# One partial sum of exponentials per half and head in place of two, in a bucketed-attention and rational-FFN kernel

## The chip, the cores and the metric

The kernel runs on one core of a Trainium2 chip. The metric is the device time of one execution in microseconds (us), as the median of several runs. Engines are called as the profile calls them: PE (TensorE), DVE (VectorE), ACT (ScalarE), POOL (GpSimd) and SP (SyncE, which issues DMAs).

## What is computed

Attention in which a query sees only the keys of its own hash bucket, and then a feed-forward layer whose nonlinearity is a quotient of polynomials. There are 4 batches, 8 heads, 768 positions and head size 64, so 3072 tokens of 512 features; the hidden layer has 2048.

```python
mask = q_bucket[:, :, :, None] == k_bucket[:, :, None, :]     # 6 sign bits of q @ proj, k @ proj
scores = scale * np.matmul(q, k.transpose(0, 1, 3, 2))
scores = np.where(mask, scores, -1000000000.0)
scores = scores - np.max(scores, axis=-1, keepdims=True)
attn = np.exp(scores)
attn = attn / (np.sum(attn, axis=-1, keepdims=True) + 1e-09)
x = np.matmul(attn, v)                                        # then heads side by side
...
h = x @ w_in
P = a[0] + a[1] * h + a[2] * h2 + a[3] * h3
Q = 1.0 + np.abs(b[0]) * np.abs(h) + np.abs(b[1]) * h2
out = (P / (Q + 1e-6)) @ w_out
```

The change concerns `np.sum(attn, axis=-1)`, the sum of the exponentials over the keys.

## The kernel before

Two heads make a pair; 16 pairs go through attention one after the other, with the work of neighbouring pairs interleaved. A pair has 12 steps: two halves of 384 queries, and in each half six key tiles of 128 keys. Keys lie on the partitions and queries along the free axis.

- `scores(p, s)` does one step. For each head PE makes two products into a PSUM tile (`pss`), ACT takes the exponential into a tile E (seven such tiles, used in turn, each for both heads), and POOL adds the tile to a running sum `acc`.
- `values(p, s)` multiplies a step's E with V into `psv`. In most pairs the six steps of a half go in one group behind its last scores.
- `maxstep(p, j)` makes maxima of the scores for a pair two places ahead: two products on PE (`psm`), one TENSOR_REDUCE on DVE (`m`). Its PSUM tiles come from the pool `ps_a`, which has two buffers; the bucket bits (`psb` on PE, compared on DVE into `mb`, for two pairs at a time) use the same two.
- `sums(p)` multiplies the running sums with a matrix of ones (`psu`), so that the sum over 128 partitions comes out on PE; a column group of 32 columns takes one head and half. ACT copies the result to `sr`.
- `low` (tiles `lo`) splits q and k into two parts for exact products, `weights(i)` prepares the FFN's weights a tile at a time (`wr`, `ws`, `wi_hi`, `wi_lo`, two tiles a pair); most of their arithmetic is on DVE.
- Behind attention comes the FFN (`psh`, `pso` on PE, `gl` on POOL); from there on POOL has no adds of exponentials.

The order on every engine is the program's own. It is written by a table: `at(p, s, f, ...)` puts a piece of work at a place counted in steps of pair p, and all pieces are issued sorted by place. The sums of a pair stand at 14.65 (pair 14: 14.69, pair 15: 16.96), that is 2.65 steps into the next pair, behind the `psm` of that step.

`PARTS` says into how many partial sums the six key tiles of a half go, `ACCS` how many buffers `acc` has. With PARTS = 2 the tiles 0 to 2 go into one sum and 3 to 5 into another. The lines that use them:

```python
        n = NT // PARTS                                        # NT = 6 key tiles
        if kt % n == 1 and heads[0] == 0:
            ACC[p, hf, kt // n] = sm.tile([P, 2, HQ], F32, tag="acc", ..., bufs=ACCS)
        if kt % n > 0:
            acc = ACC[p, hf, kt // n]
            x = EXP[p, s - 1] if kt % n == 1 else acc
            for h in heads:
                engine = nc.vector if h and late >= LAST["share"] else nc.gpsimd
                engine.tensor_tensor(out=acc[:, h, :], in0=x[:, h, 0:HQ], in1=e[:, h, 0:HQ], op=ALU.add)
...
        for k in range(PARTS):                                 # in sums(p)
            for hf in range(2):
                ...
                    nc.tensor.matmul(ps[o : o + 32, 0:HQ], ones, acc[:, h, :], start=(k == 0), stop=(k == PARTS - 1))
```

From the last step of pair 14 on (`late >= LAST["share"]`), DVE adds head 1 and POOL only head 0.

Of the kernel before, what the change touches and what calls it, by code (L numbers as in the profile page):

```python
# [34 lines left out]
BIG = 2.0 ** 60  # L35
CLAMP = 2.0 ** 40
PINNED = ("tensor", "vector", "scalar", "gpsimd", "sync")
PARTS = 2
ACCS = 5

MID = dict(
    group=6, values=[0.66, 0.05], values_out=[0.69, 0.06],
# [132 lines left out]
def attention(ctx, tc, nc, raw, ps_b, tail, tokens, early, operands_to_terms, ffn, load, QF, KF, v, w_in, w_out, wo_d, ident, cst, ones, prj,  # L175
# [180 lines left out]
    def scores(p, s, heads=(0, 1)):  # L356
# [13 lines left out]
        if both is not None:  # L370
            for h in heads:
                nc.scalar.activation(e[:, h, 0:HQ], both[:, h, 0:HQ], AF.Exp, scale=1.0 / 8.0)
        n = NT // PARTS
        if kt % n == 1 and heads[0] == 0:
            ACC[p, hf, kt // n] = sm.tile([P, 2, HQ], F32, tag="acc", name=f"acc{p}_{hf}_{kt // n}", bufs=ACCS)
        if kt % n > 0:
# [25 lines left out]
    def sums(p):  # L402
        ps = ps_b.tile([P, 512], F32, tag="s", bufs=3, name=f"psu{p}")
        for k in range(PARTS):
            for hf in range(2):
                acc = ACC.pop((p, hf, k))
                for h in range(2):
                    o = 64 * h + 32 * hf
                    nc.tensor.matmul(ps[o : o + 32, 0:HQ], ones, acc[:, h, :], start=(k == 0), stop=(k == PARTS - 1))
        ACC[p] = tail.tile([P, DM], F32, tag="sr", name=f"sr{p}")[:, 0:HQ]  # L410
# [437 lines left out]
```

## Time and profile before

| | |
|---|---|
| time of the runs | 924.08 us median of 3 (923.99 to 924.12) |
| span of the profiled execution, first to last instruction | 921.5 us |
| time around the span, median less span | 2.6 us |
| PE busy | 915.5 us, 99% |
| DVE busy | 841.5 us, 91% |
| ACT busy | 653.8 us, 71% |
| POOL busy | 426.3 us, 46% |

The profiled execution's own device time isn't listed apart from the runs, so its span stands for it. A row of the timeline gives start, length, engine, line, operation, what is written and what is read, how many instructions are merged, and in brackets the idle time of the engine before it with what ended it. Instructions are all recorded at line 95, a helper, so rows are told apart by their tiles (buffer numbers left out). A matmul in full fp32 precision appears as two records, and the ends of matmuls are modelled, so PE rows are read by their starts.

### The profile page before, as it was taken

The page shows a single profiled execution, that of the slowest core. Times are in us where ns is not written, and L with a number is a line of the kernel's source. Part 1 is how long each engine was busy: PE and PEld are TensorE (multiplying, and loading weights), DVE is VectorE, ACT ScalarE, POOL GpSimd, SP SyncE. Part 2 cuts the span into 40 slices and gives each one's busy share as a digit, 9 for nine tenths or more (in the row PEclk, how much of TensorE's full clock was granted, in tenths as well). Part 3 has the DMA queues.
Part 4 walks back from the last instruction along what each step waited for, and adds up shares of the span by engine and source line. Part 5 has one row for each costly group of instructions (what it writes and reads, how often), then busy time and mean ns, then how long its engine had stood idle before and what let it go on. Part 6 is the DMA issues. An engine that isn't in the chain of part 4 may idle for free.

```text
span 921.5 us, 13665 instructions
## 1 busy us (share of the span) xinstructions
PE 915.5 (99%) x4671; PEld 699.2 (76%) x4671; DVE 841.5 (91%) x1022; ACT 653.8 (71%) x1227; POOL 426.3 (46%) x363
## 2 busy tenths in 40 slices
PE   9999999999999999999999999999999999999998
PEld 5567767676767676678888888888888888888886
DVE  6799989999899899788998999999999989998997
ACT  7467777777777776976767677767676777667664
POOL 7577777677777777712222222222222222322221
PEclk9999999999999999999999999999999999999999
DMA  7877878787878778555403000400040013001001
GB/s 205 210 214 224 234 205 240 219 236 214 240 209 235 199 213 242 158 191 163 138 1 108 31 1 1 137 1 0 1 137 1 1 43 95 1 1 46 1 0 47
DMA packets 51242, 111.57 MB, mean 121 GB/s; under 512 B 9346, under 2 KB 20214, under 8 KB 51172
## 3 DMA queue, kind: packets, MB, share of 16 engines
q1 hardware_dynamic: 50740, 110.47, 40.7%
q8 instruction: 37, 0.61, 0.3%
q14 instruction: 33, 0.27, 0.1%
q10 hardware_dynamic: 432, 0.23, 0.1%
HBM read 56.82 MB, written 21.17 MB: 85 GB/s over the span
## 4 chain that ended last, share of the span: by engine, by line
PE 99%; DVE 1%; issue 0%; ACT 0%; DVEq 0%
PE psh L95 28%; PE pso L95 28%; PE pss L95 15%; PE psv L95 14%; PE psm L95 8%; PE psu L95 2%; PE psb L95 1%; PE psw L95 1%; PE pst L95 0%; PE pst_None L95 0%; PE psb_first L95 0%; DVE m L95 0%; DVE ws L95 0%; DVE k L95 0%; DVE mb L95 0%
## 5 line engine op out<-in xcount | busy, mean ns | idle before, releaser
L95 POOL TENSOR_TENSOR gl<-c,gh 128x512 fp32r<-128x512 f32 x95 | 135.8, 1429 | 384.9 <-ACT gh L95 374.8
L95 PE MATMUL pso<-wo,gh 128*128 128x512 f32 x768 | 235.9, 389 | 0.0
L95 DVE TENSOR_REDUCE m<-psm 128x1 f32<-128x768 f32 x192 | 181.3, 953 | 28.7 <-PE psm L95 20.1
L95 ACT ACTIVATE E<-pss 128x384 f32<-128x384 f32 x384 | 167.1, 492 | 41.5 <-PE pss L95 33.5
L95 POOL TENSOR_TENSOR acc<-E,E 128x384 f32<-128x384 f32 x124 | 147.2, 1206 | 92.1 <-ACT E L95 92.1
L95 PE MATMUL pss<-q,k 128*128 128x384 f32 (+2 forms) x768 | 171.0, 346 | 0.2
L95 PEld LDWEIGHTS pso<-wo,gh 128*128 128x128 f32 x768 | 144.1, 188 | 29.9
L95 ACT ACTIVATE h<-psh 128x512 f32<-128x512 f32 x96 | 57.4, 598 | 133.1 <-PE psh L95 133.0
L95 PEld LDWEIGHTS pss<-q,k 128*128 128x128 f32 (+2 forms) x768 | 134.5, 190 | 21.3 <-issue 8.0
L95 PE MATMUL psh<-xh,wi_hi 128*128 128x512 f32 x384 | 149.6, 390 | 0.0
L95 PE MATMUL psh<-xl,wi_hi 128*128 128x512 f32 x384 | 149.4, 389 | 0.0
L95 PE MATMUL psh<-xh,wi_lo 128*128 128x512 f32 x384 | 149.4, 389 | 0.0
L95 PE MATMUL pso<-wo,gl 128*128 128x512 f32 x384 | 148.9, 389 | 0.0
L95 DVE SCALAR_TENSOR_TENSOR c<-c,ab,r 128x512 f32<-128x512 f32 x96 | 138.7, 1444 | 0.0
L95 POOL TENSOR_TENSOR acc<-acc,E 128x384 f32<-128x384 f32 x123 | 132.0, 1093 | 3.8 <-ACT E L95 3.4
L95 PE MATMUL psv<-E,v 128*64 128x385 f32 x768 | 131.9, 492 | 0.0
L95 PE MATMUL psm<-k,q 76*128 76x384 f32 (+1 forms) x384 | 101.0, 345 | 0.5 <-ACT q L95 0.2
L95 PEld LDWEIGHTS psv<-E,v 128*64 128x64 f32 x768 | 52.0, 137 | 65.1 <-issue 62.4
L95 DVE SCALAR_TENSOR_TENSOR w<-h,absb,w 128x512 f32<-128x512 f32 x96 | 72.8, 758 | 15.5 <-ACT w L95 15.2
L95 PEld LDWEIGHTS psh<-xh,wi_hi 128*128 128x128 f32 x384 | 72.0, 188 | 16.1 <-issue 1.2
L95 PEld LDWEIGHTS psh<-xl,wi_hi 128*128 128x128 f32 x384 | 72.1, 188 | 15.0
L95 PEld LDWEIGHTS pso<-wo,gl 128*128 128x128 f32 x384 | 72.1, 188 | 15.0
(77 smaller groups left out, 1212.9 us busy)
## 6 DMA issues: line engine op xcount, KB each, us to landing
q<-q SPq DMA_DIRECT2D x45, 192.0 KB
k<-k SPq DMA_DIRECT2D x45, 192.0 KB
wr<-w_in SPq DMA_DIRECT2D x16, 512.0 KB
wr<-w_out SPq DMA_DIRECT2D x16, 512.0 KB
wo_d<-wr SPq DMA_DIRECT2D x16, 512.0 KB
wo<-wo_d SPq DMA_DIRECT2D x16, 512.0 KB
qkf<-qT SPq DMA_DIRECT2D x16, 384.0 KB
qkf<-kT SPq DMA_DIRECT2D x16, 384.0 KB
```

What stands on the lines that cost most here:

```text
L95: return self.tc.keep_in_program_order(issue(*args, **kwargs))
```

## The change

`PARTS` becomes 1 and `ACCS` 3. All six key tiles of a half go into one sum, by five adds for each half and head in place of four, and `sums` makes one product for each half and head in place of two.

```diff
-PARTS = 2
-ACCS = 5
+PARTS = 1
+ACCS = 3
```

On PE, this is the order at the sums of pair 6 before. In `acc6_1_0` the numbers are pair, half and partial sum, and "x2" stands for both heads; `psm8` are maxima for pair 8 and `pss7` scores of pair 7.

```order
L95 MATMUL psm8_8_2343<-k1_8_2045,q1_8_1990 128x384 x2
L95 MATMUL psu6_2348<-acc6_0_0_2036,ones_80 32x384 x2
L95 MATMUL psu6_2348<-acc6_1_0_2195,ones_80 32x384 x2
L95 MATMUL psu6_2348<-acc6_0_1_2116,ones_80 32x384 x2
L95 MATMUL psu6_2348<-acc6_1_1_2248,ones_80 32x384 x2
L95 MATMUL pss7_3_0_2364<-q1_7_1717,k1_7_1771 128x384
```

And this is the same place of the changed kernel:

```order
L95 MATMUL psm8_8_2333<-k1_8_2037,q1_8_1982 128x384 x2
L95 MATMUL psu6_2338<-acc6_0_0_2028,ones_80 32x384 x2
L95 MATMUL psu6_2338<-acc6_1_0_2184,ones_80 32x384 x2
L95 MATMUL pss7_3_0_2350<-q1_7_1711,k1_7_1765 128x384
L95 MATMUL pss7_3_0_2350<-q2_7_1941,k2_7_1942 128x384
```

Nothing moved on PE: the four products of the second partial sums are gone, and the neighbours are as they were.

On POOL, these are the adds of pair 6 before, E0 to E6 being the seven tiles of exponentials:

```order
L95 TENSOR_TENSOR acc6_0_0_2036<-E2_149,E3_150 128x384 x2
L95 TENSOR_TENSOR acc6_0_0_2036<-acc6_0_0_2036,E4_151 128x384 x2
L95 TENSOR_TENSOR acc6_0_1_2116<-E5_152,E6_153 128x384 x2
L95 TENSOR_TENSOR acc6_0_1_2116<-acc6_0_1_2116,E0_147 128x384 x2
L95 TENSOR_TENSOR acc6_1_0_2195<-E1_148,E2_149 128x384 x2
L95 TENSOR_TENSOR acc6_1_0_2195<-acc6_1_0_2195,E3_150 128x384 x2
L95 TENSOR_TENSOR acc6_1_1_2248<-E4_151,E5_152 128x384 x2
L95 TENSOR_TENSOR acc6_1_1_2248<-acc6_1_1_2248,E6_153 128x384 x2
```

And these are the adds of pair 6 in the changed kernel:

```order
L95 TENSOR_TENSOR acc6_0_0_2028<-E2_149,E3_150 128x384 x2
L95 TENSOR_TENSOR acc6_0_0_2028<-acc6_0_0_2028,E4_151 128x384 x2
L95 TENSOR_TENSOR acc6_0_0_2028<-acc6_0_0_2028,E5_152 128x384 x2
L95 TENSOR_TENSOR acc6_0_0_2028<-acc6_0_0_2028,E6_153 128x384 x2
L95 TENSOR_TENSOR acc6_0_0_2028<-acc6_0_0_2028,E0_147 128x384 x2
L95 TENSOR_TENSOR acc6_1_0_2184<-E1_148,E2_149 128x384 x2
L95 TENSOR_TENSOR acc6_1_0_2184<-acc6_1_0_2184,E3_150 128x384 x2
L95 TENSOR_TENSOR acc6_1_0_2184<-acc6_1_0_2184,E4_151 128x384 x2
L95 TENSOR_TENSOR acc6_1_0_2184<-acc6_1_0_2184,E5_152 128x384 x2
L95 TENSOR_TENSOR acc6_1_0_2184<-acc6_1_0_2184,E6_153 128x384 x2
```

The fourth tile of a half (E5, then E4) was not added by itself before, but together with the fifth; now every tile after the first has an add of its own, at the place of its step.

## The prediction

> **What bounds the kernel now.** I read the page first (busy shares and the chain), then one window over twelve pairs, then the PE timeline around one sum of exponentials.
>
> ```profile
> PE 915.5 (99%) x4671; PEld 699.2 (76%) x4671; DVE 841.5 (91%) x1022; ACT 653.8 (71%) x1227; POOL 426.3 (46%) x363
> PEclk9999999999999999999999999999999999999999
> PE 99%; DVE 1%; issue 0%; ACT 0%; DVEq 0%
> ```
>
> PE is busy all the time, at a full granted clock, and the chain that ended last is 99% PE. The 46% of POOL (GpSimd) is an average over two stages. The stage that matters is attention; this window runs from the sums of pair 1 to those of pair 13.
>
> ```profile
> 75.58:357.24 281.66, 281.66 (x1741) 198.32 (x1740) 253.82 (x292) 206.52 (x451) 213.47 (x193) 1.00 0.79 223
> ```
>
> Columns: window, then busy time of PE, PEld, DVE, ACT, POOL. By twelfths a pair takes 23.47 us. PE fills it, DVE works 21.15 of it (2.32 idle) and GpSimd 17.79 (5.68 idle). So time taken from PE is worth its full length until DVE or GpSimd has no idle time left, and both are nearer to that here than the page's shares say.
>
> **What is removed.** The PE timeline at the sums of pair 4 (the third row is from a narrower window, the last from the groups):
>
> ```profile
> 146.60 1.50 PE L95 MATMUL psu<-acc,ones 128*32 128x384 f32 x16
> 148.03 0.80 PE L95 MATMUL pss<-q,k 77*128 77x384 f32 x3
> 147.59 0.51 PE L95 MATMUL psu<-acc,ones 128*32 128x384 f32 x4
> L95 PE MATMUL psu<-acc,ones 128*32 128x384 f32 x256 | 24.0, 492 | 0.1
> ```
>
> Sixteen matmul records (eight products of two records) run in four rounds of four, one in each 32-column group. The rounds start from 146.60 to 147.59, so 0.33 apart; the next scores begin at 148.03. The change keeps two rounds: 2 x 0.33 = 0.66 less a pair, say 0.65. Half of the whole group (24.0 / 2 = 12.0 us over 16 pairs) is the other bound, 0.75 a pair, but entering and leaving the group isn't halved. I take 16 x 0.65 = **10.4 us**, with 12.0 as the ceiling. Weight loads for the removed products lie beside the matmuls.
>
> **What is added: GpSimd.** A half and head has five adds instead of four, so a pair has 20 instead of 16: four of its eight `E+E` become `acc+E`, and four `acc+E` come new. The groups give the mean prices:
>
> ```profile
> L95 POOL TENSOR_TENSOR acc<-E,E 128x384 f32<-128x384 f32 x124 | 147.2, 1206 | 92.1 <-ACT E L95 92.1
> L95 POOL TENSOR_TENSOR acc<-acc,E 128x384 f32<-128x384 f32 x123 | 132.0, 1093 | 3.8 <-ACT E L95 3.4
> ```
>
> Four more adds at the mean of both, 1.15, make 17.79 + 4.6 = 22.4 us of GpSimd in a pair that PE would do in 23.47 - 0.65 = 22.82. It fits, with 0.4 to spare; the break-even price of an added add is (22.82 - 17.79) / 4 = **1.26 us**. Where the adds go is seen in GpSimd's timeline over two halves, with the PE row of pair 6's sums:
>
> ```profile
> 181.96 1.97 POOL L95 TENSOR_TENSOR acc<-E,E 128x384 f32<-128x384 f32 x2 [3.47 <-ACT E L95]
> 187.62 2.46 POOL L95 TENSOR_TENSOR acc<-acc,E 128x384 f32<-128x384 f32 x2
> 192.58 3.17 POOL L95 TENSOR_TENSOR acc<-E,E 128x384 f32<-128x384 f32 x2 [2.51 <-ACT E L95]
> 200.16 2.46 POOL L95 TENSOR_TENSOR acc<-acc,E 128x384 f32<-128x384 f32 x2
> 204.85 2.01 POOL L95 TENSOR_TENSOR acc<-E,E 128x384 f32<-128x384 f32 x2 [2.23 <-ACT E L95]
> 193.63 1.50 PE L95 MATMUL psu<-acc,ones 128*32 128x384 f32 x16
> ```
>
> The idle time stands between the halves: 3.47, 2.51, 2.23. The second half of pair 6 ends at 190.08, and its sums start on PE at 193.63: 3.55 of slack. With two adds more (1.97 without interference, 3.17 at the dearest) it ends at 192.05 to 193.25, still ahead of its sums, and ahead of the next half's first E at 192.58 in the likely case. The first half of pair 7 ends at 202.62 and then at about 204.7, against 204.85. So no queue builds up from pair to pair, and PE doesn't wait at the sums: cost nothing, covered by the 3.55. An E buffer is written again seven steps later, more than a half's six, so ScalarE isn't held. Three ACC buffers serve two live sums and one being made; the one used again was read by the sums half a pair earlier. The smaller pool moves later tiles in SBUF; its cost I put at nothing, since the first w_out tile is wanted only four FFN steps on.
>
> **What is slowed: DVE.** In GpSimd's idle time VectorE prepares weights. Here is one such step without GpSimd, the same under it, and the spread of these operations (lowest, median, highest in ns):
>
> ```profile
> 178.97 0.68 DVE L95 SCALAR_TENSOR_TENSOR ws<-ws,wr 128x512 int32<-128x512 int32 x1
> 201.82 1.35 DVE L95 SCALAR_TENSOR_TENSOR ws<-ws,wr 128x512 int32<-128x512 int32 x1
> L95 DVE SCALAR_TENSOR_TENSOR ws<-ws,wr x32: 676/1232/1469, 44.8 to 393.8; 128x512 int32<-128x512 int32 x32
> L95 DVE CUSTOM_DVE_ANT_0 ws<-wr,ws x32: 668/681/1296, 48.3 to 394.6; 128x1024 uint16<-128x1024 uint16 x32
> L95 DVE TENSOR_SCALAR wr<-wr x32: 414/469/1099, 32.1 to 393.3; 128x512 int32<-128x512 int32 x32
> L95 DVE TENSOR_TENSOR wr<-ws,wr x16: 680/1414/1498, 55.2 to 396.0; 128x512 fp32r<-128x512 f32 x16
> ```
>
> The two engines hold each other up. Two of each of the first three run in a pair. Bounds of what DVE gains in work: nothing, if they all still find gaps; and 2 x (1.469 - 0.676 + 1.296 - 0.668 + 1.099 - 0.414) = 4.2 us, if each goes from its lowest to its highest. Some are under GpSimd already, and four of 5.68 idle us go away; I take a fifth of that, 0.8 a pair: 21.15 + 0.8 = 22.0 of 22.82. DVE still fits on average. It doesn't at one place, the sums that are followed by the bucket bits `psb` (pair 5; DVE rows, then PE):
>
> ```profile
> 166.22 0.69 DVE L95 SCALAR_TENSOR_TENSOR ws<-ws,wr 128x512 int32<-128x512 int32 x1
> 167.44 0.96 DVE L95 TENSOR_REDUCE m<-psm 128x1 f32<-128x768 f32 x1 [0.54 <-PE psm L95]
> 171.52 0.95 DVE L95 TENSOR_TENSOR lo<-qkf,k 128x768 fp32r<-128x768 f32 x1
> 172.38 1.01 DVE L95 TENSOR_SCALAR mb<-psb,cst 128x768 fp32r<-128x768 f32 x1
> 173.55 3.09 DVE L95 TENSOR_REDUCE m<-psm 128x1 f32<-128x768 f32 x3 [0.16 <-PE psm L95]
> 170.78 1.47 PE L95 MATMUL psb<-qkf,prj 128*32 128x384 f32 x16
> 174.07 0.52 PE L95 MATMUL psm<-k,q 76*128 76x384 f32 x2
> ```
>
> From 167.44 to 173.39 DVE has no idle time. The maxima `psm` at 174.07 take the PSUM buffer that `mb` leaves at 173.39: 0.68 of slack, which PE's 0.65 uses up. Whatever makes DVE late here is then lost on PE. The `ws` at 166.22 ran alone and is covered now: about 0.67 later (1.35 - 0.68), its neighbours some tenths, less 0.54 of idle time ahead of 167.44: 0.4 late. Six sums (odd pairs 1 to 11) have `psb` behind them: 6 x 0.4 = **2.4 us** lost, between 0 and 6 x 0.65 = 3.9.
>
> **Pair 14.** Here DVE takes the last add of head 1, and the sums come close behind:
>
> ```profile
> 375.13 1.00 POOL L95 TENSOR_TENSOR acc<-acc,E 128x384 f32<-128x384 f32 x1
> 375.20 1.35 DVE L95 TENSOR_TENSOR acc<-acc,E 128x384 f32<-128x384 f32 x1 [1.87 <-POOL acc L95]
> 377.36 1.50 PE L95 MATMUL psu<-acc,ones 128*32 128x384 f32 x16
> ```
>
> Two GpSimd adds more stand ahead of that DVE add, which begins near 377.2 and ends near 378.5; PE would want it at 377.4 or so. PE waits about a microsecond, the saving there is gone: **1.0 us** lost (0.3 to 2). Queued behind it on DVE is weight work, which nothing on PE wants soon. Pair 15 has two more DVE adds, at most 1.35 each, well ahead of its sums in the FFN.
>
> **The sum.** 10.4 - 2.4 - 1.0, and 13 x 0.15 = 2.0 for places where two queues at 96 to 98% of their pair catch on each other (0 to 0.4 each; a guess between these): 5.0 us. The profiled span is 921.5; 916.5 after. The median of the runs, 924.08, lies 2.6 above the span, work outside the first and last instruction that the change leaves: **919.1 us**. A measurement here tells 0.2%, 1.9 us, from no change.
>
> **Rivals.** *Full gain:* DVE's slowing is absorbed and only pair 14 loses: about 9 to 10 us, 914.5. For it: DVE's 2.3 idle us a pair; against: the 0.68 at `mb`. *No change:* DVE is a microsecond late at the odd sums and several tenths at the others, and the 10.4 is eaten: 922.5 to 925.5.
>
> *Slower, GpSimd becomes the bound.* Past 1.26 us for an added add, GpSimd's lateness grows from pair to pair until PE waits at every sums for the last add. The dearest adds of the rows cost 3.17 / 2 = 1.59: 17.79 + 4 x 1.59 = 24.15 a pair, 0.68 over 23.47, over 13 pairs 9 us: 933. For it: 0.4 us of margin only; against: the added adds mostly fall where the old ones cost 0.97.
>
> *Slower, DVE is shut out.* This row shows an operation held through three adds:
>
> ```profile
> 210.05 2.88 DVE L95 TENSOR_TENSOR wi_lo<-ws,wi_hi 128x512 fp32r<-128x512 f32 x1
> ...
> L95 DVE TENSOR_TENSOR wi_lo<-ws,wi_hi x16: 677/1053/2885, 70.4 to 392.7; 128x512 fp32r<-128x512 f32 x16
> ```
>
> The median of this operation is 1.05 (below). If GpSimd's longer unbroken runs did this once a pair, DVE would have 21.15 + 0.8 + 1.8 = 23.75 us to do: 0.28 over, 13 x 0.28 = 4 us slower, 928. It happened once in the whole trace.
>
> *Slower, full exclusion.* If GpSimd's adds (0.98 each, from 1.97 for two) and VectorE's operations on SBUF (lowest prices 0.68, 0.67, 0.41, 0.68 and 0.95 for `lo`, two of each a pair: 6.8) could not overlap at all, a pair would take 20 x 0.98 + 6.8 = 26.4 us, 2.9 more than now, 38 us over 13 pairs: 962. Against it stands what VectorE did under the eight adds from 192.58 to 202.62:
>
> ```profile
> 192.48 0.68 DVE L95 CUSTOM_DVE_ANT_0 ws<-wr,ws 128x1024 uint16<-128x1024 uint16 x1
> 193.94 0.94 DVE L95 TENSOR_TENSOR lo<-qkf,q 128x768 fp32r<-128x768 f32 x1
> 197.29 1.08 DVE L95 TENSOR_TENSOR lo<-qkf,k 128x768 fp32r<-128x768 f32 x1
> 200.02 0.47 DVE L95 TENSOR_SCALAR wr<-wr 128x512 int32<-128x512 int32 x1
> 200.41 1.48 DVE L95 TENSOR_TENSOR wr<-ws,wr 128x512 fp32r<-128x512 f32 x1
> ```
>
> At lowest prices these are 3.7 us. The adds took 10.04, 2.2 more than 8 x 0.98: six tenths of it was paid, and in the gaps between halves nothing is. The Trainium skill, "SBUF — State Buffer", section "Who interferes with whom", has the rule: a VectorE instruction with two SBUF inputs and a GpSimd instruction that reads SBUF block each other, the later for the whole of the earlier. By that rule the sum is this rival's; the trace agrees in kind (0.68 against 1.35 for `ws`), and not in full size.
>
> **Chances.** Forecast (gain 3 to 8) 0.52; full gain 0.13; no change 0.17; GpSimd bound 0.09; DVE shut out 0.06; full exclusion 0.03. Faster by over 0.2%: the first two and a little of the third's edge, 0.67; within: 0.15; slower: 0.18. The forecast's own range is 916 to 921.5. For eight in ten the range goes from the full gain, 914.3, into the milder slower cases, 927.
>
> **What would show it.** `psu` at 128 records and about 13 us; GpSimd some 22 us a pair with gaps under 1.5 us between halves; `ws` medians higher, DVE 22 us a pair; PE still at over 99% in the window with a pair of 23.0 to 23.2; at the odd sums PE waiting for `mb`; at pair 14 `psu` stretched by a wait for DVE's add. It is wrong if PE waits for `acc` at the sums of ordinary pairs, or if `m` is late at most `psm`.

## The result, and the profile after

| | before | after |
|---|---|---|
| median of the runs, us | 924.04 (923.24 to 924.12, 4 runs) | 936.78 (931.36 to 944.37, 4 runs) |
| ratio | | 1.0148, 95% interval 1.0100 to 1.0196 |
| span of the profiled execution, us | 921.5 | 929.6 |

The change made the kernel slower, by 1.5% in the ratio of the runs and 1.4% (12.7 us) between the medians. The forecast was 919.1 us, some 5 us faster, and its range for eight in ten ended at 927, so the result lies outside. The runs of the changed kernel also lie 13 us apart, where those before lie within 1 us. The profile shown is that of the fastest run, so it shows less of the loss than the median does.

First the page of the changed kernel: busy times, and the chain that ended last.

```profile
PE 915.4 (98%) x4543; PEld 694.9 (75%) x4543; DVE 858.9 (92%) x1024; ACT 651.1 (70%) x1227; POOL 494.6 (53%) x425
PE 86%; DVE 7%; DMA 3%; issue 2%; SPq 1%; ACT 1%; POOL 0%; DVEq 0%; ACTq 0%
```

PE has 128 matmul records less and still the same busy time (915.5 us before); the chain, 99% PE before, now runs 7% over DVE. POOL stands at 0% of it, so PE hardly waits for GpSimd itself.

The sums of pair 4 on PE, and the scores behind them:

```profile
147.89 0.85 PE L95 MATMUL psu<-acc,ones 128*32 128x384 f32 x8
148.67 0.97 PE L95 MATMUL pss<-q,k 77*128 77x384 f32 x4
```

From the first product to the next scores it is 0.78 us, where it was 1.43: the 0.65 of the forecast. The next view has the twelve pairs that the prediction counted by, and behind them the stretch from pair 13's sums to the first FFN product behind pair 15's sums.

```profile
77.16:359.86 282.70, 278.99 (x1646) 193.41 (x1645) 266.16 (x292) 204.69 (x450) 267.46 (x240) 1.00 0.78 221
359.86:411.61 51.75, 48.45 (x248) 31.01 (x247) 41.10 (x48) 35.32 (x77) 31.93 (x29) 0.93 0.44 137
```

The twelve pairs take 282.70 us, 1.04 more than before, though twelve sums save 7.8: 8.8 us are lost there, 0.74 a pair. DVE does 266.16 / 12 = 22.2 us a pair (22.0 was forecast) and GpSimd 22.3 (22.4 was forecast). The second stretch took 46.19 before and takes 51.75, though it has three sums, which save 1.95: 7.5 us are lost there. PE is idle in 3.3 of it, and the mean granted clock in it is 0.93. Up to pair 1's sums it is 1.58 later than before (77.16 against 75.58), 2.2 lost with one sum saved. The FFN takes as long as before. So the profiled run lost 18.5 us in all: 10.4 to be saved and 8.1 more of span.

Where PE stops, it is for DVE most of all, and then for the exponentials. These are waits of PE's weight loads and matmuls in the changed kernel (us in total, times, longest), and then the first three of them in the kernel before:

```profile
PEld psm L95 <- DVE m L95: 11.0, 24, 1.9
PEld pss L95 <- ACT E L95: 6.9, 12, 1.5
PEld psb L95 <- DVE m L95: 5.2, 7, 1.5
PE psm L95 <- DVE m L95: 2.8, 4, 1.6
```

```profile
PEld psm L95 <- DVE m L95: 4.5, 12, 0.6
PEld pss L95 <- ACT E L95: 1.8, 6, 0.6
PEld psb L95 <- DVE m L95: 0.3, 1, 0.3
```

Weight-load waits of `psm` went from 4.5 to 11.0 us, the longest from 0.6 to 1.9. And DVE is late because its operations on SBUF stand behind GpSimd's adds. The lowest, median and highest time of each in the changed kernel:

```profile
L95 DVE SCALAR_TENSOR_TENSOR ws<-ws,wr x32: 679/1348/1497, 45.2 to 403.4; 128x512 int32<-128x512 int32 x32
L95 DVE CUSTOM_DVE_ANT_0 ws<-wr,ws x32: 669/730/1451, 48.7 to 404.2; 128x1024 uint16<-128x1024 uint16 x32
L95 DVE TENSOR_SCALAR wr<-wr x32: 409/847/1269, 32.6 to 402.9; 128x512 int32<-128x512 int32 x32
L95 DVE TENSOR_TENSOR wi_lo<-ws,wi_hi x16: 689/1006/4506, 71.1 to 402.3; 128x512 fp32r<-128x512 f32 x16
```

`wr` has a median of 0.85 us where it was 0.47, `ws` 1.35 where it was 1.23. One `wi_lo` took 4.5 us; its median, 1.01, is no higher than before (1.05). In all, the first three groups are busy 18.6 us longer than before, and DVE as a whole 17.4. Its 192 maxima `m`, which read PSUM, took 950 ns each, as before (953).

PE's longest wait, at pair 13: DVE's rows, PE's, and GpSimd's unbroken run of adds.

```profile
355.87 1.08 DVE L95 TENSOR_SCALAR wr<-wr 128x512 int32<-128x512 int32 x1
356.98 1.40 DVE L95 SCALAR_TENSOR_TENSOR ws<-ws,wr 128x512 int32<-128x512 int32 x1
358.31 0.94 DVE L95 TENSOR_REDUCE m<-psm 128x1 f32<-128x768 f32 x1
359.18 1.44 DVE L95 CUSTOM_DVE_ANT_0 ws<-wr,ws 128x1024 uint16<-128x1024 uint16 x1
360.55 1.77 DVE L95 TENSOR_TENSOR y<-xl,xh 128x768 f32<-128x768 f32 x1
362.24 3.68 DVE L95 TENSOR_REDUCE m<-psm 128x1 f32<-128x768 f32 x4
```

```profile
363.24 0.62 PE L95 MATMUL psm<-k,q 76*128 76x384 f32 x2 [1.63 <-DVE m L95]
```

```profile
354.40 4.71 POOL L95 TENSOR_TENSOR acc<-acc,E 128x384 f32<-128x384 f32 x4
359.07 2.42 POOL L95 TENSOR_TENSOR acc<-E,E 128x384 f32<-128x384 f32 x2
361.46 8.78 POOL L95 TENSOR_TENSOR acc<-acc,E 128x384 f32<-128x384 f32 x8
```

All four SBUF operations of DVE are well above their lowest times (0.41, 0.68 and 0.67 us for the weights, 0.95 for `y` of 768 columns) while GpSimd runs without a gap; the maximum between them isn't. PE stands 1.63 us for a PSUM buffer. Then comes something that the prediction had not at all: the granted clock (the last column but two) around this wait, and in windows of 3.3 us behind it and behind another place at 394 us.

```profile
361.30:363.20 1.90, 0.30 (x2) 0.00 (x0) 1.90 (x3) 1.88 (x4) 1.90 (x3) 1.00 1.00 205
365.10:368.40 3.30, 3.30 (x12) 1.84 (x12) 3.30 (x4) 2.19 (x5) 3.30 (x4) 0.50 0.81 239
395.80:399.10 3.30, 3.30 (x13) 2.04 (x13) 3.20 (x3) 2.91 (x8) 3.07 (x4) 0.50 0.80 236
```

After the wait of 1.63 us PE was back at work for 1.8 us when the clock went down to half; at 394 us it had stood 1.14 us and, after some work, 0.53, and the clock went down about half a microsecond later. Both times it stayed there for at least 3.3 us. If PE does half its work in that time, each costs some 1.65 us, and two make 3.3 of the 8.1 us by which the spans differ: an estimate. The longest run differs by this, too: the mean granted clock was 0.996 in the run of 931.36 us and 0.986 in that of 944.37, so (1 - clock) x span is 3.7 us in the one and 13.2 in the other, 9.5 of the 13.0 us between them. It doesn't explain the two runs between: they are 4.4 and 6.4 us longer than the fastest, of which the same reckoning gives the clock 1.9 and 1.0.

### The profile page after: what moved, and what is told of

Read it like the earlier page. It is cut to its first block, busy times and chain, and to the rows that moved or that the text cites. A ratio compares the mean times of both kernels' runs of the same rounds, so it can differ in the third digit from the quotient of the medians.

```text
span 929.6 us, 13658 instructions
## 1 busy us (share of the span) xinstructions
PE 915.4 (98%) x4543; PEld 694.9 (75%) x4543; DVE 858.9 (92%) x1024; ACT 651.1 (70%) x1227; POOL 494.6 (53%) x425
## 4 chain that ended last, share of the span: by engine, by line
PE 86%; DVE 7%; DMA 3%; issue 2%; SPq 1%; ACT 1%; POOL 0%; DVEq 0%; ACTq 0%
PE psh L95 28%; PE pso L95 28%; PE psv L95 10%; PE pss L95 10%; PE psm L95 6%; DVE m L95 2%; DMA q<-q 2%; DVE lo L95 1%; SPq L95 1%; DVE ws L95 1%; DVE wi_lo L95 1%; DMA k<-lo 1%; PE psu L95 1%; PE psb L95 1%; PE psw L95 1%
## 5 line engine op out<-in xcount | busy, mean ns | idle before, releaser
L95 POOL TENSOR_TENSOR acc<-acc,E 128x384 f32<-128x384 f32 x247 | 270.8, 1129 | 6.8 <-ACT E L95 6.1
L95 DVE TENSOR_REDUCE m<-psm 128x1 f32<-128x768 f32 x192 | 179.0, 950 | 20.1 <-PE psm L95 15.0
L95 PE MATMUL pss<-q,k 128*128 128x384 f32 (+2 forms) x768 | 173.0, 349 | 3.4 <-ACT E L95 1.9
L95 PE MATMUL psm<-k,q 76*128 76x384 f32 (+1 forms) x384 | 103.2, 350 | 3.9 <-DVE m L95 2.8
L95 POOL TENSOR_TENSOR acc<-E,E 128x384 f32<-128x384 f32 x62 | 74.6, 1221 | 31.1 <-ACT E L95 30.9
L95 PEld LDWEIGHTS psh<-xh,wi_hi 128*128 128x128 f32 x384 | 72.1, 188 | 16.1 <-ACT r L95 0.6
L95 PEld LDWEIGHTS psh<-xh,wi_lo 128*128 128x128 f32 x384 | 72.1, 188 | 15.0
```

Of the source, the lines that this page charges most:

```text
L95: return self.tc.keep_in_program_order(issue(*args, **kwargs))
```

## The experiments

**The halves of the change apart.** Adds alone: five adds, but PE multiplies each sum twice, with ones of 0.5.

```diff
-    nc.vector.memset(ones, 1.0)
+    nc.vector.memset(ones, 0.5)
...
-        for k in range(PARTS):
+        for k in range(2):
             for hf in range(2):
-                acc = ACC.pop((p, hf, k))
+                acc = ACC[p, hf, 0]
...
-                    nc.tensor.matmul(ps[o : o + 32, 0:HQ], ones, acc[:, h, :], start=(k == 0), stop=(k == PARTS - 1))
+                    nc.tensor.matmul(ps[o : o + 32, 0:HQ], ones, acc[:, h, :], start=(k == 0), stop=(k == 1))
```

> Five adds on GpSimd for each half and head, but PE's sums as long as before: each sum is multiplied twice with ones of 0.5. Theory A (GpSimd's longer runs hold DVE up on SBUF, DVE is late for PE's buffers, and long waits of PE halve its clock): all the waits and none of the saving, so slower than the change itself or equal, 935 to 950 us. Theory B (the shorter sums make PE outrun a DVE that was full already; the added adds are harmless): 922 to 927 us.

Measured: 939.11 us, ratio 1.0174 (1.0159 to 1.0188). One of its runs took 937.84 us at a mean granted clock of 1.000: there the waits alone, without time at half clock, cost 14 us. Products alone, on the kernel before:

```diff
-        for k in range(PARTS):
+        for k in range(1):
...
-        nc.vector.scalar_tensor_tensor(out=z, in0=z, scalar=S * TINY, in1=s, op0=ALU.max, op1=ALU.add)
+        nc.vector.scalar_tensor_tensor(out=z, in0=z, scalar=1.0, in1=s, op0=ALU.max, op1=ALU.add)
```

> Four adds as before, but the sums multiply only the first partial sum of each half and head (the second is left out of the result, and the floor under the sums is 1.0, so that no row divides by zero). Theory A: PE's saving of 16 x 0.65 = 10.4 us comes through with small losses, 913 to 917 us. Theory B: PE only meets DVE sooner, 921 us or more.

Measured: 914.92 us, ratio 0.9907 (0.9894 to 0.9919). So the shorter sums are worth 8.8 us by themselves, near the 10.4 that the prediction gave, and theory B falls as it was written. The added adds cost 15.4 us without any shortening on PE. The halves make 6.6 us together, though, and the change lost 12.7: some 6 us, against an interval of over 4 either way, come only when both are there. That PE with shorter sums comes sooner to a DVE that is late would do this; no run shows it.

**As many adds, but less of GpSimd's time.**

```diff
-                engine.tensor_tensor(out=acc[:, h, :], in0=x[:, h, 0:HQ], in1=e[:, h, 0:HQ], op=ALU.add)
+                w = HQ if kt == 1 else 288
+                engine.tensor_tensor(out=acc[:, h, 0:w], in0=x[:, h, 0:w], in1=e[:, h, 0:w], op=ALU.add)
...
-        nc.vector.scalar_tensor_tensor(out=z, in0=z, scalar=S * TINY, in1=s, op0=ALU.max, op1=ALU.add)
+        nc.vector.scalar_tensor_tensor(out=z, in0=z, scalar=1.0, in1=s, op0=ALU.max, op1=ALU.add)
```

> The change with five adds, but the second to fifth take 288 of the 384 columns (the rest is left out of the sum; the floor under the sums is 1.0), so that a pair's 20 adds occupy GpSimd about as long as 16 full ones. Theory A: GpSimd's gaps are back and with them most of the gain, 914 to 920 us. If the number of adds, the longer dependent chain on one sum or the buffers were the cause: 930 us or more. Theory B: 922 us or more.

Measured: 915.85 us, ratio 0.9918 (0.9905 to 0.9931), 0.9 us more than the products alone. So the number of adds, the longer chain on one sum, and three buffers do next to no harm; the length of the adds does. With 336 columns in place of 288:

> As the narrow adds before, with 336 of 384 columns in the second to fifth add (the rest is left out of the sum; the floor under the sums is 1.0). Theory A with a loss that grows as GpSimd's idle time goes: between 916 and 937, near 922 us. With a loss that sets in only when the idle time is all but gone: 915 to 918 us.

Measured: 926.42 us, ratio 1.0034 (1.0021 to 1.0047). 288, 336 and 384 columns give 915.9, 926.4 and 936.8: some 10 us for each 48 columns. The loss grows with the width of the adds and doesn't wait until GpSimd's idle time is used up.

**Where in the kernel.** One sum for pairs 0 to 13 alone:

```diff
+def parts(p):
+    return 1 if p < NPAIR - 2 else 2
...
-        n = NT // PARTS
+        n = NT // parts(p)
...
-        for k in range(PARTS):
+        for k in range(parts(p)):
...
-                    nc.tensor.matmul(ps[o : o + 32, 0:HQ], ones, acc[:, h, :], start=(k == 0), stop=(k == PARTS - 1))
+                    nc.tensor.matmul(ps[o : o + 32, 0:HQ], ones, acc[:, h, :], start=(k == 0), stop=(k == parts(p) - 1))
```

> One sum for pairs 0 to 13, two as before for pairs 14 and 15. In the profile of the change 6.2 of the loss stand in pairs 14 and 15, and pairs 0 to 13 lose about what they save. Theory A, with the loss spread over all pairs: 922 to 928 us. Rival C (only the last two pairs, where DVE shares the adds, are at fault): 914 to 919 us.

Measured: 939.04 us, ratio 1.0164 (1.0142 to 1.0187). Rival C falls, and my range of 922 to 928 is missed too: 14 of 16 pairs lose as much as all. (This kernel keeps five `acc` buffers; the change with five, further down, takes 943.1.) Its profile shows the extreme of the mechanism. DVE's first step towards the reciprocals, GpSimd, and PE:

```profile
167.27 5.08 DVE L99 TENSOR_SCALAR rz<-rs 128x48 f32<-128x48 f32 x1
```

```profile
167.87 4.44 POOL L99 TENSOR_TENSOR acc<-acc,E 128x384 f32<-128x384 f32 x5
172.67 2.42 POOL L99 TENSOR_TENSOR acc<-E,E 128x384 f32<-128x384 f32 x2 [0.36 <-ACT E L99]
```

```profile
177.69 0.65 PE L99 MATMUL psm<-k,q 76*128 76x384 f32 x2 [4.26 <-DVE m L99]
```

```profile
178.20:181.50 3.30, 3.30 (x25) 0.94 (x24) 3.30 (x5) 1.10 (x2) 0.00 (x0) 0.50 1.04 244
```

An operation on 48 columns stands 5.08 us and ends at 172.35, within 0.1 us of the end of GpSimd's run of five adds (172.31). GpSimd then rests 0.36 us. All of DVE's queue comes late, PE waits 4.26 us for a maximum, and behind the wait its clock is halved. This end is the same everywhere: in all the traces here, each `rz` that took over 2.4 us ends 0.04 or 0.05 us after a run of adds, and each `wi_lo` over 2.8 us ends 0.55 after one.

For the even pairs 0 to 12 alone (`return 1 if p % 2 == 0 and p < NPAIR - 2 else 2`):

> One sum for the even pairs 0 to 12 only, two for the others. Theory A (GpSimd's longer runs of adds hold VectorE up, and PE waits for VectorE): half the saving, 4.5 us, and the losses of seven pairs, which have no bucket bits behind their sums: 918 to 930 us. If the loss came from one sum anywhere in the kernel and not from GpSimd's load, it would be half of the change's 13: 929 to 931 us.

Measured: 922.34 us, ratio 0.9986 (0.9977 to 0.9995). This version is faster than the kernel before by a seventh of a per cent. Seven sums save 4.5 us and keep a little over 1. No profile of an execution near that time was kept, so it has no row in the table below.

**Buffers.** `ACCS = 5` in the changed kernel:

> The change with five acc buffers in place of three. Theory A: no difference from the change, 930 to 945 us. Rival D (three buffers make GpSimd wait for PE's sums, or the moved tiles matter): 914 to 925 us.

Measured: 943.13 us, ratio 1.0227 (1.0208 to 1.0245). More buffers don't help, so rival D falls. They even make it some 6 us slower than the change, and the intervals don't touch; why stays open. In its profile `rz` is held for over 5 us twice, and PE waits some 4.3 us behind each, where the profile of the change has no such `rz`.

**Fewer, longer holds.** One add for both heads:

```diff
+            if len(heads) == 2 and late < LAST["share"]:
+                nc.gpsimd.tensor_tensor(out=acc, in0=x[:, :, 0:HQ], in1=e[:, :, 0:HQ], op=ALU.add)
+                return
             for h in heads:
```

> The change, with one add of 2 x 384 columns for both heads in place of two of 384. From the 1.82 us of GpSimd's subtractions of 768 columns a pair's adds take some 1.5 us less of GpSimd, but each holds VectorE up for longer. Theory A with GpSimd's idle time deciding: 918 to 930 us. If the length of one hold decides: 935 us or more.

Measured: 964.44 us, ratio 1.0447 (1.0432 to 1.0461). The same edit on the kernel before:

> The kernel before, with one add of 2 x 384 columns for both heads in place of two of 384: GpSimd has less to do, PE the same. If the length of one hold on VectorE decides: slower than before by 10 us or more, 934 us. If GpSimd's share of busy time decides: 920 to 926 us.

Measured: 932.10 us, ratio 1.0090 (1.0075 to 1.0105). That is 8.4 us slower, short of the 10 or more expected if the length of one hold decides, but outside the 920 to 926 us expected if GpSimd's busy share does. GpSimd's busy time by itself isn't the cause, then. The pages of the narrow adds, of this edit on the changed kernel, and of it on the kernel before:

```profile
PE 907.0 (99%) x4543; PEld 693.8 (76%) x4543; DVE 840.5 (92%) x1024; ACT 651.8 (71%) x1227; POOL 438.8 (48%) x425
```

```profile
PE 926.1 (96%) x4543; PEld 698.9 (73%) x4543; DVE 892.5 (93%) x1024; ACT 654.0 (68%) x1227; POOL 439.6 (46%) x278
```

```profile
PE 917.5 (99%) x4671; PEld 699.0 (75%) x4671; DVE 857.3 (92%) x1022; ACT 654.7 (70%) x1227; POOL 390.5 (42%) x246
```

GpSimd is busy 438.8 and 439.6 us in kernels of 915.9 and 964.4 us; DVE, which has the same operations in both, 840.5 and 892.5. In the third GpSimd is the least busy of all kernels here, and DVE has 15.8 us more than before. A hold is now as long as an add of 768 columns, 1.8 us in the mean in place of 1.1. With this edit on the changed kernel, `lo` and `wr` took:

```profile
L95 DVE TENSOR_TENSOR lo<-qkf,q x13: 1557/1564/1743, 51.9 to 369.1; 128x768 fp32r<-128x768 f32 x13
L95 DVE TENSOR_SCALAR wr<-wr x32: 410/1719/1951, 32.3 to 437.5; 128x512 int32<-128x512 int32 x32
```

In the change itself this `lo` took 0.94 to 1.52 us (median 0.95), and `wr` had the median 0.85.

**More, shorter holds.** The products alone, with each add in two of 192 columns:

```diff
-                engine.tensor_tensor(out=acc[:, h, :], in0=x[:, h, 0:HQ], in1=e[:, h, 0:HQ], op=ALU.add)
+                for c in (slice(0, HQ // 2), slice(HQ // 2, HQ)):
+                    engine.tensor_tensor(out=acc[:, h, c], in0=x[:, h, c], in1=e[:, h, c], op=ALU.add)
```

> The products alone (four adds, half the products, the second partial sum left out), with every add made as two of 192 columns. By the medians of 802 ns for 288 columns and 1012 for 384, 32 adds take 32 x 0.59 = 18.9 us a pair, as much as the adds of width 336 (18.6), but one hold is half as long. If the length of one hold decides: 914 to 918 us. If GpSimd's busy share decides: 924 to 928 us.

Measured: 929.42 us, ratio 1.0054 (1.0036 to 1.0071): 14.5 more than the products alone, and 3.0 more than width 336, so above both expectations. The length of one hold doesn't decide alone either. The profile tells why: `ws` got quicker, and `wi_lo` is now shut out in nine of sixteen cases. Behind the times is one of them, with the adds that end its hold.

```profile
L95 DVE SCALAR_TENSOR_TENSOR ws<-ws,wr x32: 679/964/1076, 45.3 to 401.8; 128x512 int32<-128x512 int32 x32
L95 DVE TENSOR_TENSOR wi_lo<-ws,wi_hi x16: 628/3953/4084, 69.4 to 400.7; 128x512 fp32r<-128x512 f32 x16
139.66 4.04 DVE L95 TENSOR_TENSOR wi_lo<-ws,wi_hi 128x512 fp32r<-128x512 f32 x1
141.03 2.12 POOL L95 TENSOR_TENSOR acc<-acc,E 128x192 f32<-128x192 f32 x4
```

Most operations get their turn early (1.08 us at most for `ws`); `wi_lo` stands until a run of adds ends.

**Less for DVE to do.** The changed kernel without VectorE's last operation on a weight tile:

```diff
-            nc.vector.tensor_tensor(out=t.bitcast(I32), in0=t.bitcast(I32), in1=lw.bitcast(I32), op=ALU.add)
```

> The change without the last addition that VectorE makes for each weight tile (32 operations ws<-wr,ws, 29.8 us busy in the profile of the change; the weights' lowest bits are left out). GpSimd and PE have the same instructions as in the change. Theory A (VectorE's lateness is what PE waits for): 915 to 926 us. If PE waited for GpSimd, for E or for its own order, VectorE's load would not matter: 932 us or more.

Measured: 931.58 us, ratio 1.0068 (1.0034 to 1.0101). 5.2 us come back, between the two expectations (915 to 926, and 932 or more) and nearer the rival's; the runs reach from 925.1 to 934.4, and the interval just touches that of the change. So this run alone doesn't part the theories. The profile helps: 29.8 us of DVE's work are gone, but its busy time fell by 13.1 only, so what is left was held 16.7 us longer. The long holds are still there, and `rz` has two more, of 4.0 and 5.1 us.

```profile
L95 DVE TENSOR_TENSOR wi_lo<-ws,wi_hi x16: 628/979/4603, 68.4 to 405.2; 128x512 fp32r<-128x512 f32 x16
```

**All of them together.** For each kernel that has all of DVE's work: its time less the time that PE's work alone allows (taken as 923.7 for long sums, and 0.65 less for each pair with a short one), beside DVE's busy time, which shows how long its operations were held.

| kernel | time | PE's work alone | lost | DVE busy |
|---|---|---|---|---|
| before | 923.7 | 923.7 | 0 | 841.5 |
| products alone | 914.9 | 913.3 | 1.6 | 840.5 |
| narrow adds, 288 | 915.9 | 913.3 | 2.6 | 840.5 |
| both heads, on before | 932.1 | 923.7 | 8.4 | 857.3 |
| narrow adds, 336 | 926.4 | 913.3 | 13.1 | 858.0 |
| the change | 936.8 | 913.3 | 23.5 | 858.9 |
| half adds, products alone | 929.4 | 913.3 | 16.1 | 860.2 |
| adds alone | 939.1 | 923.7 | 15.4 | 862.2 |
| pairs 0 to 13 | 939.0 | 914.6 | 24.4 | 864.4 |
| change, five buffers | 943.1 | 913.3 | 29.8 | 866.0 |
| both heads, on the change | 964.4 | 913.3 | 51.1 | 892.5 |

The loss goes broadly with DVE's held time and not with GpSimd's load: GpSimd is busy 390.5 us in the fourth row and 438.8 in the third. It isn't proportional, since what counts is where the hold falls, and since the profiled run isn't the median one.

## Why the prediction was wrong, point by point

- *PE's saving, 16 x 0.65 = 10.4 us.* Right: with the products alone it is 0.65 at the sums of every pair, and 8.8 us in the time. In the change it shows in full at the even pairs, and pair 14 gives it back. At the odd sums, from the first product to `psb`, it was 1.31 us before and is 0.67 only twice in six; the others take 1.00 to 1.69, because `psb` waits:

```profile
265.52 0.85 PE L95 MATMUL psu<-acc,ones 128*32 128x384 f32 x8
267.21 1.18 PE L95 MATMUL psb<-qkf,prj 128*32 128x384 f32 x12 [0.84 <-DVE m L95]
```

- *GpSimd's and DVE's work a pair, 22.4 and 22.0 us.* Right: 22.3 and 22.2. The price of an add, 1.15, holds too (1.13 and 1.22 in the groups). That PE wouldn't wait at the sums for GpSimd holds as well: one weight-load wait of 0.5 us in the whole trace.
- *The bucket-bit sums, 2.4 us.* Of the right kind, but too small. The wait that it named, of `psm` for `mb`, went from 0.2 us to 2.2 in seven waits. What it didn't have is that `m` is late at `psb` already, 5.2 us of weight-load waits for 0.3 before. Taken from one `psu` to the next, the six stretches behind odd sums lose 5.2 us, 0.87 each.
- *Pair 14, 1.0 us.* At the sums, right in kind, and within its 0.3 to 2: 0.6 us of the saving is gone, with 1.38 us to the next scores for 1.43 before, and a weight load waits there for DVE's add:

```profile
382.51 1.45 PE L95 MATMUL psu<-acc,ones 128*32 128x384 f32 x8
383.13 0.14 PEld L95 LDWEIGHTS psu<-acc,ones 128*32 128x32 f32 x2 [0.28 <-DVE acc L95]
383.89 2.38 PE L95 MATMUL pss<-q,k 77*128 77x384 f32 x12
```

- *"13 x 0.15 = 2.0 for places where two queues at 96 to 98% of their pair catch on each other".* This step failed: the term was mis-sized, four times too small where it can be seen alone. Both queues fitted on average, as I had worked out, and I read from this that the catching would be small. The six stretches behind even sums, which have no bucket bits, lose 3.7 us, 0.61 each in place of 0.15. The twelve pairs together lose 8.8 us in the fastest run, where 2.4 and 12 x 0.15, 4.2 in all, were set down. So a pair takes 23.56 us, and not the 23.0 to 23.2 named as a sign. A full queue gives a hold back slowly: with the 0.8 us of idle time a pair that the sum left to DVE, a hold of 4.5 us takes some five pairs (an estimate). And PE comes back to these buffers every 1.06 us within a series of maxima (203.32, 204.38 and 205.44 before), with 0.68 of slack at the one place measured.
- *The rival "DVE is shut out", 0.06.* This was the mechanism at its worst, priced too low (928) and thought a single accident. In the profile of the change it is still one case, 4.51 us; most of the loss there comes from operations that are held for less. In other kernels it is common, and it strikes `rz` there, which is no weight operation.
- *Omitted: the clock.* No term of the sum let a wait of PE cost more than its length. The Trainium skill, "TensorE: Matmul & The Clock Gate", section "HAM oscillation — how this bites in real kernels", warns of gaps over some 3.4 us; here 1.63 us of waiting was followed by half clock, so by the rule none of it would have come, and the measurement decides. Not every such wait has it behind: after 1.75 us in the kernel with the adds alone (at 273.15) and 1.62 us in that with five buffers (at 373.60) the clock stayed at 1.00 for the 4 us that followed.
- *Omitted: pairs 14 and 15.* In the stretch from 359.86 to 411.61 the loss, 7.5 us, isn't only pair 14's, and this is the largest gap between the sum and the run. "Queued behind it on DVE is weight work, which nothing on PE wants soon" failed here. DVE stands for GpSimd's late add, by the order of the program and not for SBUF (1.87 us before). Behind its weight work comes `y` of the tokens; ScalarE stands in order for `y` (0.39 us at this place before), and the exponentials wait behind it. DVE, ScalarE and PE:

```profile
381.72 1.35 DVE L95 TENSOR_TENSOR acc<-acc,E 128x384 f32<-128x384 f32 x1 [3.50 <-POOL acc L95]
```

```profile
392.39 0.62 ACT L95 CAST xh<-y 128x512 fp32r<-128x512 f32 x1 [2.08 <-DVE y L95]
```

```profile
394.12 0.62 PE L95 MATMUL pss<-q,k 77*128 77x384 f32 x2 [1.14 <-ACT E L95]
```

- *Full exclusion, by the Trainium skill's rule on the shared port, 962 us.* Not for the change, whose operations mostly still find their turn. The Trainium skill's rule ("SBUF — State Buffer", section "Who interferes with whom") has the kind right, and more than I granted it: the price to be reckoned isn't the sum of lengths but who waits. With adds of both heads in one, the time came to 964; that this is near the rival's 962 is chance, since the rival reckoned with other adds.

Left open: why some operations of DVE get in behind one add and others stand through five. In the traces it struck `wi_lo` and `rz` most, at the end of a pair's second half, when GpSimd runs its adds without a gap; no run varied that alone. Open, too, are why the two halves of the change cost more together, and what the slower runs of the change lost beyond the profiled one. The share of the clock in the median run is an estimate from the granted clocks.

## What to carry to other kernels

Two engines that read SBUF together are not two queues with their own shares: before you give GpSimd work beside a nearly full VectorE, ask what an operation of VectorE waits for, one add or the rest of a run, and what then waits for VectorE. A sum of busy times that just fits says nothing about that; the price is in the holds against the slack of the engine that bounds. And on a kernel that is all TensorE, look at the granted clock behind each wait of one to two microseconds: here some had a stretch at half clock behind them and others not.

## What the runs showed of the hardware

- A VectorE operation on SBUF can stand through a whole unbroken run of GpSimd's adds: 5.08 us for an operation on 48 columns, ended with the run, and about 4.0 us for nine of sixteen `wi_lo` when the adds were halved in length and doubled in number, each ended 0.55 us after the run.
- GpSimd adds of both heads, 768 columns in place of twice 384, took GpSimd less time (439.6 us busy for 494.6) and the changed kernel 28 us more.
- After a wait of PE of 1.63 us the granted clock went to 0.50 within 2 us and stayed there for 3.3 us or more, while PE was working; no such stretch lies inside the attention stage of the kernel before. Waits of 1.75 and 1.62 us in two other kernels had none behind them.
